# Waits by tile instead of by pool at the seams of a one-core adaLN block, forward and backward

## Chip, core and metric

The kernel runs on one core of one Trainium2 chip. A core has four compute engines that matter here (TensorE, called PE; VectorE, DVE; ScalarE, ACT; GpSimd, POOL), a fifth, SyncE (SP), that only issues transfers, and 16 DMA engines that move data between HBM and the on-chip SBUF. Matmuls write to PSUM, which has eight banks of 2 KB for each of the 128 partitions. The metric is the device time of one execution in microseconds (us), as the median of several runs.

## The reference

One transformer block whose two branches are modulated by a condition vector c, and its gradients. In bf16, with S = 2048 tokens, D = 512, 32 heads of 16, F = 1792:

```python
def forward(x, wqkv, wo, w1, b1, w2, b2, c, w_mod):
    sa, ca, ga, sb, cb, gb = split(silu(c) @ w_mod, 6)     # six rows of 512
    h = layernorm(x) * (1 + ca) + sa
    x = x + ga * attention(h, wqkv, wo)                    # softmax(q k^T / 4) v, 32 heads, no mask
    h = layernorm(x) * (1 + cb) + sb
    x = x + gb * (relu(h @ w1 + b1) ** 2 @ w2 + b2)
    return x

out, vjp = jax.vjp(forward, ...)
return out, *vjp(grad_out)       # out and the nine gradients
```

## The kernel before, in words

The work runs in five stages, one after the other, on tokens in four chunks of 512.

*Prep* (function `prep`, PSUM pool `psP`): loads, layer norm of x, the modulation rows `modbc`, and the projections of the first heads' q, k and v, with `pk`, `pm` and others as PSUM tiles and `vP` as an evicted piece of v that goes into `vaug` (v with a column of ones).

*Attention forward* (the loop over `u` in `range(NF + 2)`, PSUM pools `psS`, `psO` and `psM`): 512 units, each of one query chunk, one group of four heads and one tile of 128 keys. PE makes scores of four heads in two pairs of banks (`psST`), ACT takes their exponential (`ET`), and two units later PE multiplies with `vaug` into `oacc`. Into these units everything else of the first three chunks is woven: projection, both halves of the MLP, their gradients, weight gradients. A dictionary `plan` holds for each unit the functions to be called in it; `at(u, f, ...)` writes an entry, and `later(k, f, ...)` puts a transfer off by k steps. All products of this kind share one PSUM bank: `mm()` takes the only tile `pm` of `psM`. `last_ds(fc)` is one of them: in units 119 to 132 it makes fourteen products of `gfT` with `w2T`, each evicted by DVE into `ds`. `racc` holds five rows, of which rows 0 and 1 get the reciprocals of rows 1 and 4 of `modbc`; SP stores them to `rows_st` in HBM. `chunk_loads` and `ffinish` end a chunk: sums `r_inv` over heads, a scaling of `O_un` into `O_c`, and transposes of `O_c` (`ptC`).

*Last chunk* (`last_chunk`, PSUM pool `psM2`): MLP forward and backward of the fourth query chunk. Weight gradients are made as chains of products into one of three banks `pc`, added to a part that was stored before and written out; the last of these chains leaves `dwlast`. `dltT` is the transposed row sum of dO times O of this chunk; `store_grad` stores it to `d_st`.

*Attention backward* (SBUF pools `phIt`, `phIe`, `phIw`, `phIs1`, `phIg`, `qz1pool`; PSUM pools `psId`, `psIx`): 8 groups of four heads by 64 units of 512 keys and 128 queries. For each unit PE makes scores again, one head at a time, into three banks (`psS_A`, `psS_B`, `psS_C`), ACT takes `E_u` from them, PE makes dP into `psD_u`, DVE multiplies the two into `dS_u`, and PE sums dv and dk in `accVK` and, by way of transposes `dsT`, dq in `dqacc`. Where PE would wait, a product named `idle` is put in, whose result isn't used.

*Last stage* (`phJlow`, `phJbig`, `phJw`, `psJt`, `psJd`, `psJw`): gradient of the first layer norm's output, of wqkv, and of the modulation.

The order of instructions on every engine is written out by hand in all these stages (`tc.manual_schedule`), with SP's and POOL's in the last one in part left to the framework. What the framework puts in everywhere are the waits between engines.

Memory is taken in pools, which are opened and closed like brackets. A pool that is opened after another was closed may get the same bytes. The framework then lets the new user wait for the old ones. By default it does so by pool: a pool that lands on bytes of closed pools waits, at the first use of any of its tiles, for all users of those pools.

Of the kernel before, what the change touches and what calls it, by code (L numbers as in the profile page):

```python
# [34 lines left out]
def kernel(  # L35
# [18 lines left out]
    DVE = nc.vector  # L54
# [17 lines left out]
    modbc = persist.tile([P, 6, D], BF, name="modbc")  # L72
# [9 lines left out]
    rows_st = dram.tile([8, D], F32, name="rows_st")  # L82
# [57 lines left out]
        for to, fro in row_loads(*args):  # L140
            SP.dma_start(out=to, in_=fro)

    vaugpool = tc.alloc_tile_pool(name="vaugp", bufs=1, side="right")
    vaug = vaugpool.tile([P, TT, H + 1, DH + 1], BF, name="vaug")
    kts = [vaugpool.tile([P, n], BF, name=f"kt_sb{i}") for i in range(2)]
    qts = [vaugpool.tile([P, 512], BF, name=f"qt_sb{i}") for i in range(2)]

    with ExitStack() as ph:
        wk = ph.enter_context(tc.tile_pool(name="phC", bufs=2))
        ffw = ph.enter_context(tc.tile_pool(name="ffw", bufs=1))  # L150
        cb = ph.enter_context(tc.tile_pool(name="phMc", bufs=1))
        att = ExitStack()
        ework = att.enter_context(tc.tile_pool(name="phCe", bufs=4))
# [116 lines left out]
        def next_chain():  # L270
            dwq.pop(0)[2]()
# [490 lines left out]
        psp = {}  # L762
# [411 lines left out]

        fqueue = list(range(QC - 1))
        with ExitStack() as ph2:
            psp["p"] = ph2.enter_context(tc.tile_pool(name="psP", bufs=1, space=bass.MemoryType.PSUM))
            with tc.manual_schedule(engines={PE.engine, ACT.engine, DVE.engine, SP.engine, POOL.engine}):
                prep()
        plan_tasks()  # L1180
        stages = [*range(4, 14), *range(4), 30, 31, *range(14, 25)]
        with ExitStack() as ph2:
            pools["s"] = ph2.enter_context(tc.tile_pool(name="psS", bufs=3, space=bass.MemoryType.PSUM))
            pools["o"] = ph2.enter_context(tc.tile_pool(name="psO", bufs=1, space=bass.MemoryType.PSUM))
            pools["mm"] = ph2.enter_context(tc.tile_pool(name="psM", bufs=1, space=bass.MemoryType.PSUM))
            with tc.manual_schedule(engines={PE.engine, ACT.engine, DVE.engine, SP.engine, POOL.engine}):
                fh[0, 0] = (qts[0], kts[0])
                for u in range(NF + 2):
                    unit[0] = u
                    run_due()  # L1190
                    if u < NF:
                        if funits[u][2] == 4 and u + TT < NF:
                            fload(*funits[u + TT][0:2])
                        fscore(u)
                    if 2 <= u:
                        fpv(u - 2)
                    if u % 4 == 2 and u // 4 < len(stages):
                        later_stage(stages[u // 4])
                    if u % 4 == 0 and 18 <= u // 4 < 32:
                        turn_weights(u // 4 - 18)  # L1200
                    count, begun_group = products[0], open_group[0]
                    for f, args in plan.pop(u, ()):
                        f(*args)
                    if u < NF - 4:
                        step(u)
                    elif dwq and u >= NF - 2:
                        next_chain()
                    if products[0] == count and not (begun_group or open_group[0]):
                        steady(u - 2)
                    if u >= NF - 7 and "L" in loads and "O" not in loads["L"]:  # L1210
                        early_finish()
                    if u == NF:
                        tiny = wk.tile([P, 1], F32, name="tiny", tag="tiny", bufs=1)
                        ACT.activation(tiny[:], onesf[:, 0:1], AF.Sqrt)
                    if not dense and fqueue and fdone and u - 2 >= fdone[0][0]:
                        fqueue.pop(0)
                        qc, rr, ou = fdone.pop(0)[1:]
                        ffinish(qc, rr, ou, chunk_loads(qc))
                while dense:
                    unit[0] += 1  # L1220
                    run_due()
                    step(unit[0])

        strm, hsets = [], []

        def head_set(i):
            strm.append(tc.alloc_tile_pool(name=f"phIs{i}", bufs=1, side="right"))
# [298 lines left out]
        keep = {}  # L1526
        final[0] = True
        with ExitStack() as ph2:
            pools["mm"] = ph2.enter_context(tc.tile_pool(name="psM2", bufs=4, space=bass.MemoryType.PSUM))
            with tc.manual_schedule(engines={PE.engine, ACT.engine, DVE.engine, SP.engine, POOL.engine}):  # L1530
                pools["rs"] = pools["mm"].tile([P, 512], F32, name="rsums", tag="rs", bufs=1)
                DVE.memset(pools["rs"][:], 0.0)
# [10 lines left out]
                for i in range(4):  # L1543
                    fetch_part(i)
                att.close()
                qzpool = tc.alloc_tile_pool(name="qzpool", bufs=1, side="right")
                qz = [qzpool.tile([P, TT, 4, 32], BF, name="qz0")]
                kpool = tc.alloc_tile_pool(name="kpool", bufs=1, side="right")
                dpool = tc.alloc_tile_pool(name="dpool", bufs=1, side="right")
                dwr = tc.alloc_tile_pool(name="dwr", bufs=1, side="right")  # L1550
# [17 lines left out]
        dwr.release()  # L1568

    KS_tok, dOs_tok = keep["KS"], keep["dOs"]  # L1570
    qz1pool = tc.alloc_tile_pool(name="qz1pool", bufs=1, side="right")
    qz.append(qz1pool.tile([P, TT, 4, 32], BF, name="qz1"))
    head_set(1)

    stg = tc.alloc_tile_pool(name="phIg", bufs=2, side="right")
    xs = {}

    def load_grads(key, i, tile_ap):
# [1 line left out]
        SP.dma_start(out=tile_ap, in_=(dQc if key == "dq" else dVKtP)[i])  # L1580

    with ExitStack() as ph:
        tpool = ph.enter_context(tc.tile_pool(name="phIt", bufs=3))
        ework = ph.enter_context(tc.tile_pool(name="phIe", bufs=4))
        wk = ph.enter_context(tc.tile_pool(name="phIw", bufs=2))
        psd = ph.enter_context(tc.tile_pool(name="psId", bufs=2, space=bass.MemoryType.PSUM))
        psx = ph.enter_context(tc.tile_pool(name="psIx", bufs=1, space=bass.MemoryType.PSUM))
# [15 lines left out]
        def at(j, f, *args):  # L1603
            todo.setdefault(j, []).append((f, args))
# [173 lines left out]
        with tc.manual_schedule(engines={PE.engine, ACT.engine, DVE.engine, SP.engine, POOL.engine}):  # L1778
# [49 lines left out]
        dq_last = hst[HG - 1]["dq"]  # L1828

    with ExitStack() as ph:  # L1830
        low = ph.enter_context(tc.tile_pool(name="phJlow", bufs=1))
        big = ph.enter_context(tc.tile_pool(name="phJbig", bufs=1))
        wk = ph.enter_context(tc.tile_pool(name="phJw", bufs=2))
        pst = ph.enter_context(tc.tile_pool(name="psJt", bufs=2, space=bass.MemoryType.PSUM))
        psd = ph.enter_context(tc.tile_pool(name="psJd", bufs=2, space=bass.MemoryType.PSUM))
        psw = ph.enter_context(tc.tile_pool(name="psJw", bufs=3, space=bass.MemoryType.PSUM))
# [168 lines left out]
        with tc.manual_schedule(engines={PE.engine, ACT.engine, DVE.engine}):  # L2005
            for i in range(2):
                rsums.append(pst.tile([P, D], F32, name="rsumJ", tag="ptq"))
            for t in range(TT):
# [4 lines left out]
                if t in (3, 5, 7, 9):  # L2013
                    i = 4 + (t - 3) // 2
# [92 lines left out]
```

## Time and profile before

| | before |
|---|---|
| median of 3 runs | 2475.41 us |
| these runs | 2471.93 to 2484.3 us |
| profiled execution, its own time | 2480.28 us |
| its span in the trace | 2478.5 us |
| mean granted TensorE clock | 0.984 |
| busy: PE, ACT | 2310.0 us, 2300.5 us |
| busy: DVE, POOL | 1845.9 us, 490.5 us |

The profile is one execution, recorded by the hardware; all its times count from the start of the span. A timeline row gives the start of an instruction (or of a run of alike ones, with xcount), its duration, engine and line, what it writes and reads, and in brackets the idle time of its engine just before it and what ended that idle time. A windows row gives, for a stretch of the span, the busy time of each engine in it, the clock that TensorE was granted (1.00 is full speed), the mean busy share of the 16 DMA engines and the rate of transfer. The page's list of chain shares follows the work that ended last backwards and says which engine held it.

### The profile page before, as it was taken

To read this page: it belongs to the slowest core of one execution; us is meant where nothing else is said; L and a number is where in the kernel's file an instruction comes from. 1 tells how busy PE (TensorE), PEld (TensorE's weight loads), DVE (VectorE), ACT (ScalarE), POOL (GpSimd) and SP (SyncE) were. 2 spreads that over 40 slices of the span, in tenths; PEclk is the share of its full clock that TensorE was granted. 3 is DMA by queue.
4 is the path that set the end of the run, shared out by engine and by line. 5 is a ranking of instruction groups with operands and counts; after the bars stand their busy time and mean duration, and the time that the engine had idled before them with its cause. 6 is when DMAs were issued, how large, how long until landed. Compare 5 with 4: busy or idle time off the path is not lost.

```text
span 2478.5 us, 49843 instructions
## 1 busy us (share of the span) xinstructions
PE 2310.0 (93%) x18908; PEld 778.3 (31%) x18994; DVE 1845.9 (74%) x2393; ACT 2300.5 (93%) x3559; POOL 490.5 (20%) x661
## 2 busy tenths in 40 slices
PE   8899899988998998889999999999999999999999
PEld 3232233323322332432233223333233332222344
DVE  6555453455445554668999999999999999999986
ACT  7999999999998999629999999999999999999964
POOL 2211222432544353201110101101011010110100
PEclk9999999999998999999999999999999999999999
DMA  4478554267647774989999999999999999999995
GB/s 148 129 170 193 175 142 101 84 173 133 91 93 155 149 138 99 233 236 175 195 196 202 209 192 206 205 211 203 201 202 206 208 203 200 204 191 221 200 260 181
DMA packets 1192304, 440.58 MB, mean 178 GB/s; under 512 B 1068284, under 2 KB 1161914, under 8 KB 1191551
## 3 DMA queue, kind: packets, MB, share of 16 engines
q1 hardware_dynamic: 1155214, 392.23, 80.6%
q0 software_dynamic: 19872, 27.09, 6.9%
q10 hardware_dynamic: 16976, 18.07, 3.1%
q8 instruction: 149, 2.44, 0.4%
q14 instruction: 93, 0.75, 0.1%
HBM read 98.83 MB, written 72.63 MB: 69 GB/s over the span
## 4 chain that ended last, share of the span: by engine, by line
ACT 41%; PE 37%; DVE 8%; issue 8%; DMA 4%; ACTq 1%; SPq 0%; POOL 0%; DVEq 0%; another core or an unknown queue 0%; POOLq 0%
ACT E_u L1634 25%; ACT ET L580 13%; PE dqacc L1736 4%; PE psST L578 3%; PE psS_A L1628 3%; PE accVK L1709 2%; ACT dsT L1821 2%; PE pm L234 2%; PE psS_B L1628 2%; PE oacc L594 2%; PE psS_C L1628 2%; PE pdh L1929 2%; PE pm L502 2%; PE pm L412 2%; PE accVK L1718 2%
## 5 line engine op out<-in xcount | busy, mean ns | idle before, releaser
L1650 DVE TENSOR_TENSOR dS_u<-psD_u,E_u 128x1024 bf16<-128x1024 f32 x1024 | 1185.6, 1218 | 76.6 <-PE psD_u L1648 25.3
L580 ACT ACTIVATE ET<-psST 128x1024 bf16<-128x1024 f32 x1024 | 941.9, 1232 | 17.5 <-PE psST L578 17.1
L1634 ACT ACTIVATE E_u<-psS_A 128x512 bf16<-128x512 f32 x768 | 507.5, 661 | 13.1 <-DMA d_st<-dltT 10.2
L1634 ACT ACTIVATE E_u<-psS_B 128x512 bf16<-128x512 f32 x768 | 501.0, 652 | 8.6 <-issue 2.4
L1648 PE MATMUL psD_u<-iv,ido 32*128 32x512 bf16 x2048 | 409.7, 388 | 0.1
L578 PE MATMUL psST<-qt_sb,kt_sb 32*128 32x512 bf16 x2048 | 314.0, 385 | 42.3 <-ACT ET L580 36.1
L1634 ACT ACTIVATE E_u<-psS_C 128x512 bf16<-128x512 f32 x512 | 332.9, 650 | 2.5 <-PE psS_C L1628 1.0
L1628 PE MATMUL psS_A<-ik,iq 32*128 32x512 bf16 x768 | 294.0, 383 | 16.5 <-ACT E_u L1634 5.8
L1628 PE MATMUL psS_B<-ik,iq 32*128 32x512 bf16 x768 | 295.4, 385 | 10.4 <-ACT E_u L1634 3.1
L1757 POOL TENSOR_TENSOR dQacc<-dQacc,dqtmp 128x512 f32<-128x512 f32 x64 | 81.2, 1269 | 849.7 <-ACT dqtmp L1752 849.7
L1628 PEld LDWEIGHTS <-iq 32*128 32x128 bf16 x2048 | 130.2, 91 | 314.0 <-issue 298.2
L1709 PE MATMUL accVK<-dS_u,qz 128*32 128x512 bf16 x2048 | 213.3, 388 | 0.6 <-DVE dS_u L1650 0.3
L594 PE MATMUL oacc<-ET,vaug 128*32 128x512 bf16 x2048 | 206.9, 394 | 3.9 <-DVE ostage L598 3.9
L1718 PE MATMUL accVK<-E_u,dOs_tok 128*16 128x512 bf16 x2048 | 204.0, 387 | 0.0
L1628 PE MATMUL psS_C<-ik,iq 32*128 32x512 bf16 x512 | 193.9, 379 | 4.4
L578 PEld LDWEIGHTS <-kt_sb 32*128 32x128 bf16 x2048 | 85.3, 91 | 321.0 <-issue 299.3
L1736 PE MATMUL dqacc<-dsT,KS_tok 128*32 128x512 bf16 x2048 | 146.1, 383 | 13.4 <-ACT E_u L1634 0.4
L252 DVE COPY part<-pm 128x512 f32<-128x512 f32 (+2 forms) x106 | 65.2, 615 | 121.2 <-PE pm L234 110.8
L1821 ACT ACTIVATE dsT<-ptT 128x1024 bf16<-128x1024 bf16 x126 | 142.3, 1130 | 8.8 <-PE ptT L1682 8.1
L1648 PEld LDWEIGHTS <-ido 32*128 32x128 bf16 x2048 | 104.8, 91 | 106.4 <-issue 100.7
L1709 PEld LDWEIGHTS <-qz 128*32 128x32 bf16 x2048 | 58.4, 94 | 178.3 <-issue 163.2
L1757 POOL TENSOR_TENSOR dQst<-dQacc,dqtmp 128x512 bf16<-128x512 f32 x31 | 39.4, 1270 | 266.5 <-ACT dqtmp L1752 256.3
(421 smaller groups left out, 2672.2 us busy)
## 6 DMA issues: line engine op xcount, KB each, us to landing
p_st<-part POOLq DMA_DIRECT2D x36, 256.0 KB, 4.6
kt_sb<-qkT_st POOLq DMA_DIRECT2D x124, 64.0 KB, 3.2
wA<-in_B_w_dram SPq DMA_DIRECT2D x28, 256.0 KB
wB<-w1T_st SPq DMA_DIRECT2D x21, 256.0 KB
wA<-w2T_st SPq DMA_DIRECT2D x21, 256.0 KB
wB<-in_B_w_dram SPq DMA_DIRECT2D x21, 256.0 KB
p_st<-part POOLq DMA_DIRECT2D x28, 192.0 KB, 4.9
p_st<-part SPq DMA_DIRECT2D x18, 256.0 KB
```

Source lines behind the costliest of these rows:

```text
L578: PE.matmul(ps[:, hi, :], kt_sb[r:r + 32, kt * P:(kt + 1) * P], qt_sb[r:r + 32, :], start=True, stop=True, tile_position=(r, 0))
L580: ACT.activation(ET[:, 2 * pair:2 * pair + 2, :], ps[:], AF.Exp, scale=SCALE)
L594: PE.matmul(oacc[32 * hq:32 * hq + 32, :], lhsT, ET[:, hq, :], start=(kt == 0), stop=(kt == TT - 1), tile_position=(0, 32 * hq), skip_grou ...
L1628: PE.matmul(psS[:], st["q"][r:r + 32, qt * P:(qt + 1) * P], st["k"][r:r + 32, kc * 512:kc * 512 + 512], start=True, stop=True, tile_positi ...
L1634: ACT.activation(bst[u][0][:, hq, :], sst.pop((u, hq))[:], AF.Exp, scale=SCALE)
L1648: PE.matmul(psD[:, hi, :], st["do"][r:r + 32, qt * P:(qt + 1) * P], st["v"][r:r + 32, kc * 512:kc * 512 + 512], start=True, stop=True, til ...
L1650: DVE.tensor_tensor(dS_u[:, 2 * pair:2 * pair + 2, :], psD[:], E_u[:, 2 * pair:2 * pair + 2, :], ALU.mult)
L1709: PE.matmul(cur["vk"][32 * hq:32 * hq + 32, :], hst[hg]["qz"][:, qt, hq, :], bst[u][1][:, hq, :], start=(qt == 0), stop=False, tile_positi ...
L1718: PE.matmul(acc[32 * hq:32 * hq + DH, :], dOs_tok[:, qt, (hg * 4 + hq) * DH:(hg * 4 + hq + 1) * DH], E_u[:, hq, :], start=False, stop=(qt ...
L1736: PE.matmul(acc[32 * hq:32 * hq + 32, :], KS_tok[:, kc * 4 + kt, h * DH:h * DH + 32], tT[:, :, hq * 4 + kt, :], start=(kt == 0), stop=(kt ...
L1757: POOL.tensor_tensor(dst2, dst, tmp[:], ALU.add)
L1821: ACT.activation(dst, pt[:], AF.Identity)
```

## The change

Two edits. The first gives every pool but the two permanent ones (`persist`, and `dram` in HBM) the argument `reuse_waits="tile"`. With it, a tile waits only for the users of those earlier tiles that lay on its own bytes (in PSUM: in its own bank), and not for all users of the closed pools. It is in 28 places; three of them:

```diff
-    vaugpool = tc.alloc_tile_pool(name="vaugp", bufs=1, side="right")
+    vaugpool = tc.alloc_tile_pool(name="vaugp", bufs=1, reuse_waits="tile", side="right")
...
-            pools["s"] = ph2.enter_context(tc.tile_pool(name="psS", bufs=3, space=bass.MemoryType.PSUM))
+            pools["s"] = ph2.enter_context(tc.tile_pool(name="psS", bufs=3, reuse_waits="tile", space=bass.MemoryType.PSUM))
...
-        ework = ph.enter_context(tc.tile_pool(name="phIe", bufs=4))
+        ework = ph.enter_context(tc.tile_pool(name="phIe", bufs=4, reuse_waits="tile"))
```

The pools are those named above, and `phC`, `ffw`, `phMc` and `phCe` (forward), `qzpool`, `kpool`, `dpool` and `dwr` (last chunk).

The second edit moves the two one-row reciprocals from units 130 and 132 to 134 and 136, and the store of their rows from unit 134 to 138:

```diff
             for r, j in enumerate((1, 4)):
-                at(130 + 2 * r, DVE.reciprocal, racc[0:1, r, :], modbc[0:1, j, :])
-            at(134, sp, rows_st[6:8, :].unsqueeze(0), racc[0:1, 0:2, :])
+                at(134 + 2 * r, DVE.reciprocal, racc[0:1, r, :], modbc[0:1, j, :])
+            at(138, sp, rows_st[6:8, :].unsqueeze(0), racc[0:1, 0:2, :])
```

The order of all other instructions on all engines is the same in the text of the kernel.

More of the change, by code (lines that the diff above doesn't have):

```diff
@@ L1176 @@
         with ExitStack() as ph2:
-            psp["p"] = ph2.enter_context(tc.tile_pool(name="psP", bufs=1, space=bass.MemoryType.PSUM))
+            psp["p"] = ph2.enter_context(tc.tile_pool(name="psP", bufs=1, reuse_waits="tile", space=bass.MemoryType.PSUM))
             with tc.manual_schedule(engines={PE.engine, ACT.engine, DVE.engine, SP.engine, POOL.engine}):
@@ L1182 @@
         with ExitStack() as ph2:
-            pools["s"] = ph2.enter_context(tc.tile_pool(name="psS", bufs=3, space=bass.MemoryType.PSUM))
-            pools["o"] = ph2.enter_context(tc.tile_pool(name="psO", bufs=1, space=bass.MemoryType.PSUM))
-            pools["mm"] = ph2.enter_context(tc.tile_pool(name="psM", bufs=1, space=bass.MemoryType.PSUM))
+            pools["s"] = ph2.enter_context(tc.tile_pool(name="psS", bufs=3, reuse_waits="tile", space=bass.MemoryType.PSUM))
+            pools["o"] = ph2.enter_context(tc.tile_pool(name="psO", bufs=1, reuse_waits="tile", space=bass.MemoryType.PSUM))
+            pools["mm"] = ph2.enter_context(tc.tile_pool(name="psM", bufs=1, reuse_waits="tile", space=bass.MemoryType.PSUM))
             with tc.manual_schedule(engines={PE.engine, ACT.engine, DVE.engine, SP.engine, POOL.engine}):
@@ L1226, in head_set @@
         def head_set(i):
-            strm.append(tc.alloc_tile_pool(name=f"phIs{i}", bufs=1, side="right"))
+            strm.append(tc.alloc_tile_pool(name=f"phIs{i}", bufs=1, reuse_waits="tile", side="right"))
             hs = {key: strm[i].tile([P, n], BF, name=f"i{key}{i}") for key in ("k", "v", "q", "do")}
@@ L1528 @@
         with ExitStack() as ph2:
-            pools["mm"] = ph2.enter_context(tc.tile_pool(name="psM2", bufs=4, space=bass.MemoryType.PSUM))
+            pools["mm"] = ph2.enter_context(tc.tile_pool(name="psM2", bufs=4, reuse_waits="tile", space=bass.MemoryType.PSUM))
             with tc.manual_schedule(engines={PE.engine, ACT.engine, DVE.engine, SP.engine, POOL.engine}):
@@ L1570 @@
     KS_tok, dOs_tok = keep["KS"], keep["dOs"]
-    qz1pool = tc.alloc_tile_pool(name="qz1pool", bufs=1, side="right")
+    qz1pool = tc.alloc_tile_pool(name="qz1pool", bufs=1, reuse_waits="tile", side="right")
     qz.append(qz1pool.tile([P, TT, 4, 32], BF, name="qz1"))
     head_set(1)
-    stg = tc.alloc_tile_pool(name="phIg", bufs=2, side="right")
+    stg = tc.alloc_tile_pool(name="phIg", bufs=2, reuse_waits="tile", side="right")
     xs = {}
@@ L1830 @@
     with ExitStack() as ph:
[L1831 to L1836, printed above, removed]
+        low = ph.enter_context(tc.tile_pool(name="phJlow", bufs=1, reuse_waits="tile"))
+        big = ph.enter_context(tc.tile_pool(name="phJbig", bufs=1, reuse_waits="tile"))
+        wk = ph.enter_context(tc.tile_pool(name="phJw", bufs=2, reuse_waits="tile"))
+        pst = ph.enter_context(tc.tile_pool(name="psJt", bufs=2, reuse_waits="tile", space=bass.MemoryType.PSUM))
+        psd = ph.enter_context(tc.tile_pool(name="psJd", bufs=2, reuse_waits="tile", space=bass.MemoryType.PSUM))
+        psw = ph.enter_context(tc.tile_pool(name="psJw", bufs=3, reuse_waits="tile", space=bass.MemoryType.PSUM))
         entry = tc.manual_schedule(engines={PE.engine, ACT.engine, DVE.engine, SP.engine})
```

24 lines of the change are left out of this document (12 added, 12 removed).

## The prediction

> **What bounds the kernel now.** I read the page first, then one table of windows, cut where the stages change hands, because the change acts only there.
>
> ```profile
> span 2478.5 us, 49843 instructions
> ...
> PE 2310.0 (93%) x18908; PEld 778.3 (31%) x18994; DVE 1845.9 (74%) x2393; ACT 2300.5 (93%) x3559; POOL 490.5 (20%) x661
> ...
> ACT 41%; PE 37%; DVE 8%; issue 8%; DMA 4%; ACTq 1%; SPq 0%; POOL 0%; DVEq 0%; another core or an unknown queue 0%; POOLq 0%
> ```
>
> PE and ACT are each busy 93% of the span, and the chain that ended last goes through them for 78%. The table of windows by stage (length, busy time of each engine, granted clock, DMA share, GB/s) shows where the other 7% lie:
>
> ```profile
> core 0: us, PE busy (x) PEld busy (x) DVE busy (x) ACT busy (x) POOL busy (x), PEclk, DMA share, GB/s
> 0.00:41.20 41.20, 30.74 (x190) 15.12 (x193) 26.82 (x79) 27.55 (x44) 13.70 (x38) 0.96 0.47 155
> 41.20:999.00 957.80, 868.40 (x6031) 287.49 (x6098) 485.24 (x954) 943.19 (x1026) 315.15 (x491) 0.99 0.61 135
> 999.00:1109.40 110.40, 97.51 (x572) 46.57 (x580) 76.98 (x180) 48.50 (x91) 13.10 (x26) 1.00 0.91 244
> 1109.40:1113.90 4.50, 0.00 (x0) 0.00 (x0) 0.00 (x0) 0.00 (x0) 0.00 (x0) 0.58 0.79 264
> 1113.90:2371.00 1257.10, 1210.92 (x11503) 377.86 (x11503) 1185.88 (x1025) 1227.58 (x2333) 147.31 (x106) 0.98 1.17 202
> 2371.00:2478.50 107.50, 102.38 (x619) 51.29 (x625) 70.95 (x157) 53.66 (x67) 1.27 (x1) 1.00 0.75 220
> ```
>
> The attention forward (41 to 999 us) is bound by ACT (943 of 958), the attention backward (1114 to 2371) by ACT, PE and DVE together (98, 96, 94%), the last stage by PE. Between last chunk and backward lie 4.50 us in which no engine does anything: that is the waiting for closed pools in its pure form. The change can give no more than the waits at the four borders (about 41, 1000, 1109 and 2371 us) plus what the reciprocals hold up.
>
> **The change part by part.** With waits by pool, the first tile of a pool that lies on released bytes waits for the last user of every pool there; with waits by tile, only for users of tiles on its own bytes (in PSUM, its own bank). These are a part of the old waits, and every engine's order stays as it was, so no wait is added; what can cost time is only what an earlier start collides with, or the clock.
>
> *Prep to forward, 41 us.* The timeline of PE and DVE:
>
> ```profile
> 41.23 0.30 DVE L834 COPY vaug<-vP 128x512 bf16<-128x512 bf16 x1
> 41.25 0.39 PE L578 MATMUL psST<-qt_sb,kt_sb 32*128 32x512 bf16 x4 [1.77 <-DVE vP L833]
> ...
> 42.66 0.69 DVE L833 CAST vP<-pm 128x512 bf16<-128x512 f32 x1 [1.12 <-PE pm L828]
> ...
> 43.40 1.02 PE L828 MATMUL pm<-wqkv_nat,h1T 128*128 128x512 bf16 x4 [0.20 <-DVE vP L833]
> ```
>
> The first scores wait 1.77 us for an eviction of the prep pool that isn't in their banks. That wait goes. What is late next: PE's product after it has to be evicted by DVE, which is occupied until 41.23 + 0.30 = 41.53; the eviction that began at 42.66 can begin there, 1.1 earlier, and the next product (43.40) follows it. I take **1.1**; bounds 0 (if ACT has enough of a backlog from other causes) and 1.77.
>
> *The reciprocals.* Two one-row reciprocals of 3.33 us each stand on DVE before and between the last evictions of the ds products:
>
> ```profile
> 281.82 3.33 DVE L1203 RECIPROCAL racc<-modbc 1x512 f32<-1x512 bf16 x1
> ...
> 285.08 0.62 DVE L1129 CAST ds<-pm 128x512 bf16<-128x512 f32 x1
> 285.75 1.02 PE L1127 MATMUL pm<-gfT,w2T 128*128 128x512 bf16 x4 [2.01 <-DVE ds L1129]
> 286.81 0.69 DVE L1129 CAST ds<-pm 128x512 bf16<-128x512 f32 x1 [1.11 <-PE pm L1127]
> 287.19 25.77 ACT L580 ACTIVATE ET<-psST 128x1024 bf16<-128x1024 f32 x28 [1.48 <-PE psST L578]
> 287.42 3.33 DVE L1203 RECIPROCAL racc<-modbc 1x512 f32<-1x512 bf16 x1
> ...
> 292.66 6.22 SPq L179 DMA_DIRECT2D wA<-in_B_w_dram  x6
> 293.48 0.96 DVE L677 RECIPROCAL r_inv<-pm 128x128 f32<-128x128 f32 x1 [2.73 <-PE psST L578]
> 294.47 4.42 DVE L621 TENSOR_TENSOR O_c<-O_un,r_inv 128x512 bf16<-128x512 bf16 x4
> ...
> 299.92 0.62 PE L350 MATMUL ptC<-identb,O_c 128*128 128x128 bf16 x8
> ```
>
> The first holds the eviction of product 12 until 285.08; there is one pm bank, so the next product waits 2.01, the scores behind it come late, and ACT, the bound here, stands 1.48. Moved behind product 13, they hold no eviction of a product. The gain is ACT's 1.48: **1.5** (0 to 2.0). What they can now hold up: the last ds eviction would end about 2 us sooner, an estimate of 285.5 from 286.81 + 0.69 less 2.01; the two then end at 285.5 + 6.66 = 292.2, and r_inv, with PE 1.5 to 2 earlier, is wanted at 291.5 to 292. At most 0.7 late, and the transposes of O_c come only at 299.92, 1.0 us after DVE's scaling has ended (294.47 + 4.42 = 298.89), which covers it; if that cover were gone, PE would stand 0.7. On SP, the row store moves behind the loads of g_c, wo_nat and x_c, which no longer wait for the second reciprocal; the store itself then waits until 292.2, and the next load behind it (wA) left at 292.66, so nothing there is later. POOL, which takes g_c, can only gain.
>
> *Forward to last chunk, 1000 us.*
>
> ```profile
> 999.98 0.81 PE L659 MATMUL pm<-wo_nat,OT 128*128 128x512 bf16 x2 [0.65 <-DVE part L252]
> 1000.17 0.48 DVE L1532 MEMSET rsums<- 128x512 f32 x1 [0.25 <-DVE part L252]
> ```
>
> PE waits 0.65 for an eviction out of another bank; DVE does that eviction and the memset anyway. I take **0.4** (0 to 0.65).
>
> *Last chunk to backward, 1109 us.*
>
> ```profile
> 1108.65 0.37 PE L1628 MATMUL psS_A<-ik,iq 32*128 32x512 bf16 x1 [0.95 <-DVE dwlast L238]
> ...
> 1108.98 0.39 PE L1797 MATMUL idle<-identb,ones_bf 128*128 128x512 bf16 x1
> ...
> 1111.85 1.72 SPq L179 DMA_DIRECT2D d_st<-dltT  x4
> ...
> 1113.92 0.60 ACT L1634 ACTIVATE E_u<-psS_A 128x512 bf16<-128x512 f32 x1 [10.22 <-DMA d_st<-dltT]
> ...
> 1114.57 0.58 PE L1628 MATMUL psS_A<-ik,iq 32*128 32x512 bf16 x1 [5.20 <-ACT E_u L1634]
> ```
>
> The first exponential waits until the store out of dltT has landed. By the tiles' sizes in the order of allocation the first E_u lies on the tail of dwbuf and on woT, the first dS_u on rT and sT, and dltT below both, so by tile it needn't wait for that store. psS_A lies in the bank of the last pc chain: its 0.95 for dwlast stays, and the score is there at 1108.65 + 0.37 = 1109.02. ACT starts 1113.92 − 1109.02 = **4.9** earlier; PE's 5.20 go with it. dltT's store then runs beside the first units.
>
> The second half of this border is the clock. Windows of all engines around it, and far behind it one more fall:
>
> ```profile
> 1110.10:1113.50 3.40, 0.00 (x0) 0.00 (x0) 0.00 (x0) 0.00 (x0) 0.00 (x0) 0.50 0.81 262
> 1113.50:1127.10 13.60, 12.18 (x61) 2.25 (x60) 8.93 (x8) 9.33 (x18) 8.80 (x5) 0.50 0.49 113
> ...
> 1195.40:1205.60 10.20, 10.20 (x66) 2.94 (x66) 6.56 (x7) 7.86 (x14) 0.00 (x0) 0.50 0.88 165
> ```
>
> and windows of the dS_u product on DVE alone, the pace of the backward (length, busy, clock, DMA share, GB/s):
>
> ```profile
> 1115.30:1137.90 22.60, 17.90 (x15) 0.74 0.73 145
> 1137.90:1195.40 57.50, 55.14 (x48) 1.00 1.16 197
> 1195.40:1217.50 22.10, 17.87 (x17) 0.77 1.00 186
> 1217.50:2370.60 1153.10, 1094.63 (x947) 0.99 1.18 203
> ```
>
> The granted clock is 0.50 from 1110.1 to 1127.1. In the first 22.60 us DVE is idle 4.70; at the normal pace (1 − 1094.63/1153.10 = 5.07%) it would be 1.15. The slow clock and the first filling cost 3.55; I count **3.3** as the clock's. With the gap closed, PE goes on from its last idle-filling product (to 1108.98 + 0.39 = 1109.37) to the second psS_A when the first exponential of 0.60 has ended, at 1109.62, so the clock should stay. Bounds: 0, if the clock falls all the same (it fell 0.7 us behind the last matmul), and 3.55.
>
> [...]
>
> *Backward to last stage, 2371 us.* The queue's own waits, and a window:
>
> ```profile
> SPq L1847 <- PE accVK L1718: 5.3, 1, 5.3
> 2375.50:2389.00 13.50, 13.45 (x169) 9.63 (x163) 8.10 (x16) 8.26 (x10) 1.27 (x1) 1.00 0.90 292
> ```
>
> SP's load of wT stands 5.3 us for the last E_u product, but PE is busy 13.45 of the 13.50 us after it with transposes and the last dq sums: that work hides the load. wT_all also lies on the dS_u buffers used last, so most of the wait stays. **0**; bound 0 to the 0.05 that PE is idle there. Were the cover gone, it would be 5.3.
>
> Sum: 1.1 + 1.5 + 0.4 + 4.9 + 3.3 = **11.2 us**. The profiled execution took 2480.28 (span 2478.5 and 1.8 around it), 4.87 over the median of the runs, 2475.41; none of the terms scales with that difference, so 2475.41 − 11.2 = **2464.2**.
>
> **The rivals.**
>
> *The clock falls at 1110 all the same.* For it: it fell 0.7 us after the last matmul, and at 1195.4 with PE busy 10.20 of 10.20, so idleness isn't its only cause. Against: from 1137.90 to 1195.40, without a pause, it was 1.00. Gain 11.2 − 3.3 = 7.9: 2467.5.
>
> *The fall at 1195 goes as well.* If that one is an after-effect of the cold start, it vanishes with it. Its price: 22.10 − 17.87 = 4.23 idle against 5.07% of 22.10 = 1.12, so 3.1. Gain 14.3: 2461.1. Against: 68 us lie between them.
>
> *The option does nothing,* because the allocator can't follow the users of these tiles one by one and keeps the pool's waits. Only the reciprocals are left: 2475.41 − 1.5 = 2473.9. Against: each border's waiting names one single instruction, so users are followed.
>
> *Slower: falls of the clock like that of 1195 become frequent.* The backward then runs on other phases of whatever grants the clock, and without a pause that stands between dense stretches. Each fall costs 3.1; three (9.3) still leave a gain, four (12.4) outweigh 11.2 and give 2476.6, eight give 2489. For it: such a fall came with PE wholly busy. Against: the clock is 0.99 over the 1153 us after it.
>
> **How the numbers follow.** The forecast has 0.44, the clock falling anyway 0.25, the second fall gone too 0.17, the option without effect 0.08, more falls 0.06. I take 0.5% (12.4 us: below 2463.0, above 2487.8) as about what a measurement of this kernel can tell from no change; the runs shown spread over 12.4 us (2471.93 to 2484.3), so a median of such runs can stand some 4 us off its case. Faster by over 0.5%: three quarters of the 0.17, some four tenths of the 0.44, a little of the 0.25: 0.33. Slower by over 0.5% needs eight falls: 0.03. The rest is 0.64. The range goes from 14.3 and upper bounds of the small terms (1.77 + 2.0 + 0.65 instead of 3.0, so 1.4 more), with the 4 us of scatter, 2456, up to the option without effect, 2474; outside lie the more falls and half of the case at its upper edge.
>
> **What would show it.** Right: the first E_u at 1109 to 1110 less what was gained before, with no wait for d_st; PEclk 1.00 in the windows from 1110 to 1127; no window without any busy engine; DVE's evictions of products 12 and 13 without a reciprocal in front, and ACT's 1.48 gone near 287; the first scores at 39.5 instead of 41.25. Wrong: a clock of 0.50 in the start of the backward (then 7.9), the first E_u still waiting for a DMA (the address is not what I worked out: then 4.9 and 3.3 go), r_inv or the transposes of O_c waiting for a reciprocal, or a mean clock in the backward below 0.98.

## The result, and the profile after

| | before | after |
|---|---|---|
| median of 22 runs each | 2475.43 us | 2468.83 us |
| these runs | 2467.43 to 2487.63 us | 2460.11 to 2480.18 us |
| profiled execution, its own time | 2480.28 us | 2464.45 us |
| mean granted clock of it | 0.984 | 0.990 |

The ratio is 0.9972, with a 95% interval of 0.9958 to 0.9985: 6.9 us faster, between 3.7 and 10.4. The two profiled executions lie 15.8 us apart, over twice as much, so the first question is which part of that the change made. The page and the windows by stage of the changed kernel (same columns as before):

```profile
span 2462.6 us, 49825 instructions
...
PE 2300.2 (93%) x18908; PEld 777.6 (32%) x18994; DVE 1846.0 (75%) x2393; ACT 2298.3 (93%) x3559; POOL 488.9 (20%) x661
```
```profile
core 0: us, PE busy (x) PEld busy (x) DVE busy (x) ACT busy (x) POOL busy (x), PEclk, DMA share, GB/s
38.60:996.60 958.00, 867.92 (x6033) 287.40 (x6099) 487.56 (x958) 943.64 (x1027) 314.36 (x491) 0.99 0.60 135
996.60:1106.30 109.70, 96.83 (x571) 46.41 (x578) 77.09 (x179) 48.16 (x90) 13.19 (x27) 1.00 0.90 242
1106.30:2358.00 1251.70, 1204.33 (x11525) 378.69 (x11523) 1187.16 (x1027) 1227.16 (x2334) 146.90 (x106) 0.99 1.18 204
2358.00:2462.60 104.60, 100.57 (x596) 50.09 (x602) 69.19 (x154) 51.84 (x65) 1.28 (x1) 1.00 0.73 218
```

No stretch without any busy engine is left between last chunk and backward. Cut at the starts of single instructions that both kernels have, the 15.84 us come from these stages (each row is the time, in us, from the mark of the row above to its own):

| up to | before | after | difference |
|---|---|---|---|
| start, first exponential ET | 41.73 | 39.06 | −2.67 |
| last ET | 954.81 | 954.91 | +0.10 |
| eviction of rsums (L1521) | 110.69 | 110.64 | −0.05 |
| first exponential E_u | 6.69 | 1.74 | −4.95 |
| 31st product dS_u | 42.27 | 40.73 | −1.54 |
| last product dS_u | 1213.22 | 1206.56 | −6.66 |
| end | 109.08 | 109.01 | −0.07 |

The border at 1109 us, now at 1106, by the timeline:

```profile
1104.61 0.68 DVE L1521 COPY r_inv<-rsums 97x512 f32<-97x512 f32 x1
1105.21 0.68 DVE L238 TENSOR_TENSOR dwlast<-pc,part 128x512 bf16<-128x512 f32 x1
```
```profile
1105.94 0.37 PE L1628 MATMUL psS_A<-ik,iq 32*128 32x512 bf16 x1 [0.86 <-DVE dwlast L238]
...
1107.00 0.37 PE L1628 MATMUL psS_A<-ik,iq 32*128 32x512 bf16 x1 [0.34 <-ACT E_u L1634]
```
```profile
1106.35 0.60 ACT L1634 ACTIVATE E_u<-psS_A 128x512 bf16<-128x512 f32 x1 [4.88 <-DMA dOT<-dOs_c]
```
```profile
1109.83 1.73 SPq L179 DMA_DIRECT2D d_st<-dltT  x4
```

The first E_u starts 0.04 us behind the end of its score (1105.94 + 0.37); the transfer that the row names landed in the same instant (in e8, where the score is earlier, E_u is too). The store of dltT is issued 3.5 us after that start, so nothing waits for it any more. What is left is the wait for dwlast in the score's own bank. Windows of all engines behind it show the clock:

```profile
1106.30:1110.90 4.60, 3.46 (x22) 0.95 (x19) 2.36 (x2) 4.09 (x8) 4.60 (x3) 1.00 0.96 319
1110.90:1117.70 6.80, 6.66 (x41) 1.25 (x35) 5.84 (x5) 4.46 (x9) 3.95 (x3) 0.50 0.57 146
```

The clock falls in the first units all the same (a fall is a stretch with a granted clock of 0.50), for 6.8 us instead of 17.0. At the first border and at the reciprocals (timelines of PE, DVE and ACT):

```profile
39.53 0.39 PE L578 MATMUL psST<-qt_sb,kt_sb 32*128 32x512 bf16 x2 [0.51 <-DVE vP L833]
...
41.67 1.02 PE L828 MATMUL pm<-wqkv_nat,h1T 128*128 128x512 bf16 x4 [0.46 <-DVE vP L833]
```
```profile
283.66 0.69 DVE L1129 CAST ds<-pm 128x512 bf16<-128x512 f32 x1 [1.11 <-PE pm L1127]
284.27 6.54 DVE L1203 RECIPROCAL racc<-modbc 1x512 f32<-1x512 bf16 x2
290.74 0.95 DVE L677 RECIPROCAL r_inv<-pm 128x128 f32<-128x128 f32 x1
```
```profile
269.56 40.66 ACT L580 ACTIVATE ET<-psST 128x1024 bf16<-128x1024 f32 x44
```

Instead of 1.77 the scores wait 0.51, for the eviction of vP, which the profile names as what released them; and ACT's run of 44 exponentials has no gap where 1.48 stood.

### The profile page after: what moved, and what is told of

The parts are those of the page before. It is cut to its first block, busy times and chain, and to the rows that moved or that the text cites. A ratio compares the mean times of both kernels' runs of the same rounds, so it can differ in the third digit from the quotient of the medians.

```text
span 2462.6 us, 49825 instructions
## 1 busy us (share of the span) xinstructions
PE 2300.2 (93%) x18908; PEld 777.6 (32%) x18994; DVE 1846.0 (75%) x2393; ACT 2298.3 (93%) x3559; POOL 488.9 (20%) x661
## 4 chain that ended last, share of the span: by engine, by line
ACT 41%; PE 36%; DVE 8%; issue 8%; DMA 4%; ACTq 1%; POOL 0%; DVEq 0%; SPq 0%; another core or an unknown queue 0%; POOLq 0%
ACT E_u L1634 25%; ACT ET L580 13%; PE dqacc L1736 5%; PE psST L578 3%; PE psS_A L1628 3%; PE accVK L1709 2%; PE pm L234 2%; ACT dsT L1821 2%; PE psS_B L1628 2%; PE oacc L594 2%; PE psS_C L1628 2%; DMA dsT<-dS_u 2%; PE pdh L1929 2%; PE pm L502 2%; PE pm L412 2%
```

## The experiments

Each kernel is compared with the kernel before, in runs on the same chip. In the traces I read the same marks as in the table above.

**e1: the reciprocals alone**

```diff
-                at(130 + 2 * r, DVE.reciprocal, ...)      # waits by pool everywhere, as before
+                at(134 + 2 * r, DVE.reciprocal, ...)
```

> Waits by pool everywhere; only the two reciprocals and their store are moved. Theory (the gain is a sum of fixed waits at the borders, on top of which falls of the clock scatter): ACT's 1.48 us near 287 us goes, the lead over the kernel before steps by about 1.5 there and nowhere else; the first E_u still waits about 10 us; the time is 1.5 us less than before, within the scatter. Rival (what counts is how many falls of the clock an execution happens to get, and any small shift of time changes that): the step at 287 is the same, but the backward is as much changed as in the full change.

Measured: 2475.73 us, ratio 0.9997 (0.9984 to 1.0010). Timelines of ACT near the reciprocals, and at the border:

```profile
275.40 30.82 ACT L580 ACTIVATE ET<-psST 128x1024 bf16<-128x1024 f32 x33
...
1111.75 0.60 ACT L1634 ACTIVATE E_u<-psS_A 128x512 bf16<-128x512 f32 x1 [10.71 <-DMA d_st<-dltT]
```

ACT's gap is gone, and the lead over the kernel before, read at the same ET, steps there from −0.3 to 1.6, by 2.0 where the theory has 1.5 (in the changed kernel from 1.2 to 2.9, by 1.7). The time shows nothing of it; an interval from −4.0 to +2.5 us can neither exclude nor confirm it.

**e2: the tile waits alone**

```diff
+                at(130 + 2 * r, DVE.reciprocal, ...)      # waits by tile everywhere, as in the changed kernel
-                at(134 + 2 * r, DVE.reciprocal, ...)
```

> Waits by tile everywhere, reciprocals where they were. Theory: leads as in the full change, about 2.3 us at 41 us and 5.0 at 1109 with some 1.6 of the clock's behind it, but no step at 287: 1.5 less gain than the full change, 5 to 7 us in the median. Rival (the reciprocals had to be moved because the tile waits make them late): the full 6.9 or more is lost.

Measured: 2466.34 us, ratio 0.9971 (0.9953 to 0.9988), so 7.2 us. ACT's gap is back (2.47 instead of 1.48; the clock is at 0.50 just there and DVE waits 1.61 instead of 1.11 for the product before it, which may make it longer), and the border at 1109 is as in the changed kernel:

```profile
287.44 18.45 ACT L580 ACTIVATE ET<-psST 128x1024 bf16<-128x1024 f32 x20 [2.47 <-PE psST L578]
```

The tile waits don't need the moved reciprocals: the rival falls. The whole gain is there without them.

**e3: tile waits behind the last chunk only**

```diff
-    qz1pool = tc.alloc_tile_pool(name="qz1pool", bufs=1, side="right")
+    qz1pool = tc.alloc_tile_pool(name="qz1pool", bufs=1, reuse_waits="tile", side="right")
...                                                     # and every pool opened after it; all before it by pool
```

> Waits by tile only for the pools opened after the last chunk. Theory: no lead until 1109, then 5.0 us at the first E_u and 1 to 2 more of the clock in the first 23 us of the backward: about 6 us in all. The granted clock is 0.50 for about 7 us behind the start instead of 17. Rival (the clock falls for as long as before): 5.0 alone.

Measured: 2467.99 us, ratio 0.9973 (0.9958 to 0.9989), 6.7 us.

```profile
1109.93 0.60 ACT L1634 ACTIVATE E_u<-psS_A 128x512 bf16<-128x512 f32 x1 [6.71 <-PE psS_C L1628]
```

From the eviction of rsums to the first E_u it takes 1.74 us, as in the full change; the clock falls at 1112.9 for 10.2 us, and the 31st product comes after 41.86 us against 42.27. This one border carries what can be measured.

**e4: tile waits up to the last chunk only**

```diff
-            pools["s"] = ph2.enter_context(tc.tile_pool(name="psS", bufs=3, space=bass.MemoryType.PSUM))
+            pools["s"] = ph2.enter_context(tc.tile_pool(name="psS", bufs=3, reuse_waits="tile", space=bass.MemoryType.PSUM))
...                                                     # and every pool opened up to dwr; reciprocals as before
```

> Waits by tile only for the pools opened up to the last chunk, reciprocals not moved. Theory: a lead of 2.3 us at 41 us, of which falls of the clock in the forward leave 1 to 2.3, up to 0.6 more at 1000 us, and nothing at 1109, where the first E_u waits about 10 us for the store out of dltT as before: 1 to 3 us in all. Rival (the tile waits of the last chunk's own pools also bring dltT's store forward): the wait at 1109 shrinks too.

Measured: 2477.81 us, ratio 1.0005 (0.9992 to 1.0018).

```profile
1110.60 0.60 ACT L1634 ACTIVATE E_u<-psS_A 128x512 bf16<-128x512 f32 x1 [11.59 <-DMA d_st<-dltT]
```

The border at 1109 is untouched (7.67 from the eviction of rsums). In the trace the lead at the ETs is 0.6 behind the first border and stays between 0.1 and 0.7 up to 770 us. It is 1.6 at the last ET, but it gets there at about 780 us, behind a fall that lasts 3.4 us instead of 6.8, and at about 850, where no border lies. The time shows no gain; the interval reaches from 2.0 faster to 4.5 slower.

**e5: PE kept working through the old wait**

```diff
                     if c == "s" and b < NU // 4:
+                        if b == 0 and i == 3:
+                            for _ in range(22):
+                                PE.matmul(idle[:], ...)       # in the kernel before
```

> The kernel before (waits by pool), with 22 products named idle put on PE in front of the fourth score, so that PE works through the wait for the store out of dltT. ACT's wait of about 10 us stays as it is. Theory of the prediction (the clock falls because PE pauses, and 3.3 us of the border are the clock's): the clock stays at 1.00 past 1110, the 30 products of dS_u after the first E_u come 1.5 to 3.3 us sooner than before (42.3 us there). Rival (the fall isn't PE's pause but the thin work of the first units, which it has in the changed kernel too): PE's clock falls about 7 us later than before, at the first units, and stays low for 7 to 10 us; the gain is 0 to 1.5. In neither case is the whole gain of the change reached.

Measured: 2475.74 us, ratio 0.9987 (0.9970 to 1.0003). Timeline of PE and windows of all engines:

```profile
1107.22 4.91 PE L1792 MATMUL idle<-identb,ones_bf 128*128 128x512 bf16 x22
```
```profile
1108.80:1117.60 8.80, 6.39 (x32) 2.20 (x32) 2.36 (x2) 4.05 (x8) 4.46 (x3) 1.00 0.60 199
1117.60:1124.40 6.80, 6.49 (x41) 1.23 (x35) 5.84 (x5) 4.50 (x9) 4.33 (x3) 0.50 0.49 92
```

With PE busy up to 1112.1 the fall comes 7.5 us later than before, at 1117.6, and the way from the first E_u to the 31st product takes 40.97 instead of 42.27: 1.3 less. That is the rival's case. The fall doesn't need the long pause, of which 1.6 us are left here (1112.1 to 1113.7); it comes in the first units.

**e6: denser first units**

```diff
-                        if b < 2 and i % 2 == 1:
-                            if nq > 0:
-                                keep_warm()
-                            elif nq < 0:
-                                PE.matmul(idle[:], ...)
+                        if b < 2 and i % 2 == 1 and nq > 0:
+                            keep_warm()
+                        elif b == 0 and nq < 0:
+                            for _ in range(2):
+                                PE.matmul(idle[:], ...)       # in the changed kernel
```

> The changed kernel with two products named idle at each exponential of the first ten instead of one at every second (15 more). Rival of e5 (thin work of the first units drops the clock): with the denser work there is no fall near 1111, and the first 30 products after the first E_u take about 39.5 us instead of 40.7: 1.2 less. Theory of the prediction (a pause of PE drops it, and the changed kernel has no pause left): the fall that it still has at 1110.9 has another cause, it comes all the same, and the added products cost up to 3 us.

Measured: 2469.01 us, ratio 0.9966 (0.9952 to 0.9980).

```profile
1107.30:1110.90 3.60, 3.60 (x21) 1.02 (x18) 1.23 (x1) 2.66 (x5) 3.60 (x3) 1.00 0.77 267
1110.90:1117.70 6.80, 6.36 (x47) 1.71 (x47) 5.66 (x5) 5.21 (x10) 4.08 (x3) 1.00 0.55 179
```

No fall: ahead of 1110.9 PE is busy 3.60 of 3.60 us here, against 3.46 of 4.60 in the changed kernel, so thin work of PE in the first units is its cause. (e12 has the same added products and no fall at the start either; the twelve other traces all have one.) But 40.38 us to the 31st product is only 0.35 less than in the changed kernel, where 1.2 were expected: either the added products cost part of what the clock gives, or there was less to give. The start is never faster than this in any trace, 1.9 below the 42.27 before. How much of the 3.55 us lost there before was the clock's can be estimated from the eight traces without products added behind the first E_u and with the old order: their starts take 40.7 to 42.3 us and grow with the time at half clock, 6.8 to 17.1 us, and a straight line through them has 40.2 at no fall. That gives some 2 us for the clock, an estimate; the rest would be the filling of the pipeline.

**e7: a step of the dq sums moved into the thin stretch**

The reason for it is the falls in the backward. These are windows of the dS_u product on DVE (length, busy and count, clock), cut at the beginnings of the falls, in the kernel before and in e1:

```profile
1277.40:1413.90 136.50, 129.56 (x113) 0.99 1.18 204
1413.90:1434.40 20.50, 18.46 (x17) 0.92 1.11 194
1434.40:1745.00 310.60, 296.27 (x257) 0.99 1.20 203
1745.00:2018.00 273.00, 259.23 (x225) 0.99 1.19 205
```
```profile
1485.60:1506.10 20.50, 18.53 (x17) 0.92 1.20 190
1506.10:1584.60 78.50, 74.13 (x65) 0.98 1.16 203
1584.60:1721.10 136.50, 129.52 (x113) 0.99 1.19 205
```

The counts, less the one cut in two at an edge, are 112, 16, 256, 224 and 16, 64, 112: all multiples of 16, which is a pair of blocks: these falls come at one point of the pair. In the nine profiles with the old order of the backward, 54 of the 60 falls there do. Two come one product earlier, behind the 63rd (the one at 1195 before, and one in e4), and four lie elsewhere, behind windows in which PE itself was busy only 33 to 67%. At the common point PE's busy share doesn't tell why; the windows of all engines before a fall and in it:

```profile
1270.60:1274.00 3.40, 3.33 (x40) 0.94 (x40) 3.40 (x4) 3.33 (x7) 1.17 (x1) 1.00 1.16 217
1274.00:1277.40 3.40, 3.28 (x29) 1.00 (x26) 3.23 (x4) 3.40 (x8) 0.10 (x1) 0.99 1.21 138
1277.40:1280.80 3.40, 3.40 (x22) 1.08 (x20) 2.79 (x3) 2.86 (x5) 0.00 (x0) 0.50 1.13 250
```

In the window before the fall PE is busy 3.28 of 3.40 us, but with 29 products instead of 40.

```diff
-            "e5 s6 q s7 D s8 e6 e7 d1 e8 s9 D d2 e9 q Q s10 "
-            "s11 e10 D q s12 e11 e12 s13 ... ").split(), "CBACBACBABABCABC"
+            "e5 s6 q s7 D s8 e6 e7 d1 e8 s9 D e9 q s10 "
+            "s11 e10 D d2 q s12 Q e11 e12 s13 ... ").split(), "CBACBACBABABACBC"
```

> The changed kernel with one step of the dq sums (8 products of 128 rows) moved one dS_u later in every second block of the backward, and the score banks relettered for it. In the six profiles so far almost all falls of the clock in the backward begin 3.4 us after the same point of a pair of blocks, where the work of PE is thinnest. Theory (falls come when the window in which the clock is judged happens to lie on that stretch; how many an execution gets is chance of phase, and makes the scatter): the falls at that point vanish, the scatter shrinks to a few us, and the median comes down by 4 to 8 us, unless the moved step costs PE waits of its own. Rival (falls have a cause outside the work of PE): as many falls as before, elsewhere; no gain.

Measured: 2579.72 us, ratio 1.0407 (1.0368 to 1.0447). PE's longest waits, and a window over the backward:

```profile
PE psS_C L1628 <- ACT E_u L1634: 26.5, 62, 0.4
PE psS_C L1628 <- ACT dqtmp L1752: 10.5, 47, 0.5
```
```profile
1149.50:2437.00 1287.50, 1209.08 (x10827) 362.21 (x10824) 1127.29 (x964) 1180.61 (x2197) 133.24 (x97) 0.92 1.07 186
```

A failure: scores in the relettered banks wait for ACT in nearly every pair of blocks (62 and 47 times in 64 pairs), and falls become many and long (0.92 over the backward). As two things were changed at once, it decides nothing on the falls' cause.

**e8: another bank for the first score**

```diff
+            psx.tile([P, 512], F32, name="first", tag="ps0")     # takes bank 4; accVK and idle get bank 5
             idle = psx.tile([P, 512], F32, name="idle", tag="accVK")
```

> The changed kernel with the bank of psS_A exchanged against that of accVK and idle, so that the first score doesn't lie in the bank of the last weight-gradient chain. Theory (what is late next at this border is that bank): psS_A's wait of 0.86 for dwlast goes, the first E_u starts 0.8 to 0.9 earlier, and no more, since the score's operands are there; 0.9 less in the trace, not to be seen in the time. Rival (another operand is late, such as the transfer that ends at the same instant): E_u starts where it did.

Measured: 2467.23 us, ratio 0.9959 (0.9943 to 0.9974).

```profile
1103.09 0.39 PE L1628 MATMUL psS_A<-ik,iq 32*128 32x512 bf16 x1
1104.02 0.38 PE L1798 MATMUL idle<-identb,ones_bf 128*128 128x512 bf16 x1 [0.54 <-DVE dwlast L238]
```

The score waits no longer, the idle product does. From the eviction of rsums (1102.69) to the first E_u (1103.51) it takes 0.8 us instead of 1.7: the theory's 0.9.

**e9, e10, e11: products added in the thin stretch**

```diff
-            "s11 e10 D q s12 e11 e12 s13 e13 D q s14 s15 e14 e15 D q "        # kernel of e8
+            "s11 e10 D q s12 e11 e12 s13 e13 D q s14 f s15 e14 e15 D q "      # e9: f is keep_warm()
+            "s11 e10 D q s12 e11 e12 s13 e13 D f q s14 f s15 e14 e15 D q "    # e11
...
-            "s5 s6 e5 f f t2 e6 s7 T2 e7 D s8 e8 D f f s9 e9 q q s10 "
+            "s5 s6 e5 f f t2 e6 s7 T2 e7 D s8 e8 D f s9 e9 q q s10 "          # e10, with e9's line
```

> The kernel of e8 with one more keep_warm product (128 rows, adds zero) in every second block of the backward, in the middle of the thin stretch: 64 products of 0.2 to 0.39 us. e7 didn't decide what makes the falls there, because the moved step made PE wait. Theory (the judged window is too thin there, by little): no falls that begin 3.4 us behind that point, the backward after its start takes 1200 us and some 0 to 13 for the added products, in every execution, so a smaller scatter. Rival (it isn't how much PE does there): falls as before, 3 to 10 of them, and 0 to 13 us more.

> As e9, but one of the four keep_warm products of the other block is taken out for it, so that PE's work is that of the kernel of e8. Theory: the falls at the old point vanish, nothing is added, about 1200 us for the backward after its start, 6 to 9 us less than the changed kernel in the median, unless the other block was kept up by just that product, and the falls come there instead. Rival: no difference to e8.

> As e9 with two products more instead of one. Theory: no falls at the old point, as e9, and twice its price for PE's time (0 to 26 us). If one product is too little to lift the stretch, this one shows it by fewer falls than e9. Rival: falls as before.

| | median, range | ratio | last 993 products of dS_u |
|---|---|---|---|
| e8 | 2467.23 (2460.85 to 2471.73) | 0.9959 (0.9943 to 0.9974) | 1205.0 us |
| e9 | 2462.22 (2459.38 to 2465.64) | 0.9943 (0.9925 to 0.9961) | 1206.4 us |
| e10 | 2462.67 (2459.02 to 2465.68) | 0.9946 (0.9928 to 0.9963) | 1206.7 us |
| e11 | 2469.07 (2467.22 to 2472.93) | 0.9974 (0.9959 to 0.9989) | 1213.5 us |

Windows of the dS_u product in e9, and in e11:

```profile
1147.80:2289.90 1142.10, 1089.49 (x942) 1.00 1.19 204
2289.90:2293.30 3.40, 1.30 (x2) 0.50 1.14 251
```
```profile
1143.00:2350.00 1207.00, 1146.28 (x988) 1.00 1.17 203
```

No fall is left at the old point. The one fall in e9 and the one in e10 begin elsewhere (PE had been busy 59% and 51% of the window before them), and in e11 there is none.

One trace without such falls could be luck, since the nine with the old order have 2 to 10 falls each. The traces tell more. All falls of a trace begin on a grid of 3.413 us (to 0.001 us), so the edges of the windows that brought no fall are known too. In the nine traces with the old order 230 edges lie behind the 16th product dS_u of a pair. All 54 that come 0.58 to 0.80 us after its start begin a fall, and none of the 176 others does. Only one edge in e9 falls into this stretch, and just at its border, so e9's trace alone shows nothing. e10 has five edges in it, e11 three, e12 (below) two, and none of these ten begins a fall. So the falls there do come from what PE does in that stretch; which property of its work counts, the number of products or another, stays open.

The runs agree. The mean granted clock is 0.990 to 0.994 in all 29 runs of e9 to e12, against 0.981 to 0.992 in the 22 of the changed kernel, and e9's and e10's runs (six each) lie within 7 us, where those 22 spread over 20. The price is the other half of the theory: e11's second product costs 7.1 us in the trace (0.11 each), and the fit below puts e9's first at some 5. Moving instead of adding shows no saving in e10 (6 above the fit), but e12, with e10's order, has 1203.3 us, only 2 above it: single traces don't settle this price.

**e12: e6, e8 and e10 together**

> The changed kernel with e6 (two idle products at each of the first ten exponentials), e8 (bank of psS_A) and e10 (one keep_warm product moved into the thin stretch) together. Theory: the three act in different places and add: E_u 0.9 us behind the eviction of rsums instead of 1.7, no fall of the clock near the start and 40.4 us instead of 41.7 to its 30th product, no falls at the thin stretch: 1.3 us less than e10, a median of about 2461, and as small a scatter as e9's and e10's. Rival (the start's clock isn't worth anything, as e6 against the changed kernel): as e10.

Measured: 2459.79 us (2458.18 to 2460.39), ratio 0.9924 (0.9910 to 0.9938).

```profile
1102.90:1113.10 10.20, 9.40 (x56) 2.50 (x55) 6.63 (x7) 7.67 (x14) 7.44 (x5) 1.00 0.75 233
1113.10:1123.10 10.00, 9.85 (x78) 2.73 (x77) 9.12 (x9) 8.64 (x17) 1.41 (x1) 1.00 1.14 184
```

It is 0.76% or some 19 us below the kernel before and clear of the changed kernel, whose interval begins at 0.9958. 1.0 us to the first E_u where 0.9 were expected, no fall at the start; but 41.4 to the 31st product, where 40.4 were expected, so the start's clock brought e12 little in its trace. Whether it is ahead of e10 is open, since their intervals overlap.

## Why the prediction was right

It gave 2464.2 and 2456 to 2474; 2468.83 lies inside, 4.6 above. The way and the main term were right, a second term was not, and the range held because the rival without that term was in it. In the traces the terms come to 0.95 + 1.7 + 0 + 4.95 + 1.5 = 9.1 instead of 11.2, of which the forward gives some back. Point by point, by its own steps:

- **The border at 1109: right.** 4.9 predicted, 4.95 measured between the same two instructions, and e3, e2 and the changed kernel all have 1.74 there. The addresses were read rightly (E_u doesn't lie on dltT), and so was what stays: the 0.95 for dwlast, now 0.86. e3 and e4 show that this border alone makes the measurable gain.
- **The clock of the start: the term that was mis-sized, 3.3 against 1.5.** The step that failed is "With the gap closed, PE goes on ... so the clock should stay", an estimate of mine from the pause of some 0.25 us that would be left there (1109.37 to 1109.62). The pause is 0.34 in the trace, and the clock fell at 1110.9 all the same, with PE busy 3.46 of 4.60 us and no pause of PE over 0.86 us between the last chunk and the fall. e5 and e6 show why: the first units are too thin in themselves (in e5 the clock falls at 1117.6 behind 6.39 busy of 8.80 us), and with them thickened the clock stays at 1.00 (e6, 3.60 of 3.60). And the 3.55 us of the first 22.60 had been put down to the clock nearly whole, though only some 2 were, by the estimate at e6. The rival "the clock falls at 1110 all the same" is what happened, and its 2467.5 is the nearest of all figures given.
- **The first border: right in size, 1.1 against about 0.95.** The second pm product starts at 41.67 instead of 43.40; 0.78 of that the profiled execution had in hand before the border, as its last pk product already ended that much earlier. That the scores would still wait 0.51 for vP wasn't foreseen.
- **The reciprocals: right in the trace (1.5 against 1.7, and 2.0 in e1), not visible in the time.** r_inv wasn't late: it follows the reciprocals at 290.74, and the transposes of O_c weren't held up.
- **The border at 1000 us: 0.4 against nothing.** PE's and DVE's short waits are gone, but PE's wait for O_c a few products later grows from 0.31 to 0.98 and takes them up: the stage takes 110.64 instead of 110.69. In the other traces it takes 108.0 to 112.2, so a single pair of traces couldn't show 0.4 either way.
- **The border at 2371: right in its worth, wrong in the wait.** That most of SP's 5.3 us would stay didn't come: the load of wT now waits 0.5, and it is the next load in the queue (qz) that waits 4.3 for the same product. The last stage takes 109.01 instead of 109.08, so the earlier load was worth nothing, as said.
- **What the forward gives back.** From the first ET to the last the changed kernel takes 0.10 more, although 1.7 of the reciprocals' are in it. 0.37 are lost at the third exponential, and its clock falls at 80.0, where the kernel before had no fall. Of the ten traces with tile waits there seven have a fall at 80 to 83 us, of the four with pool waits one (e3): whether the change brings it stays open.

The rest of the 15.8 us is chance. In the backward after its start the two profiled executions differ by 6.66 us; the clock stood at 0.50 for 37.5 us of it before and 17.1 after. Over the nine profiles with the old orders (e7 and e9 to e12 left out) the length follows this time:

| | half clock, us | last 993 products, us |
|---|---|---|
| e2 | 6.8 | 1201.0 |
| e8 | 13.7 | 1205.0 |
| after | 17.1 | 1206.6 |
| e4 | 23.9 | 1211.4 |
| e5, e1 | 30.7, 30.7 | 1211.8, 1213.5 |
| e3, e6 | 34.1, 34.1 | 1212.1, 1211.6 |
| before | 37.5 | 1213.2 |

A straight line through them has 1199.8 us at no fall and 0.39 us per us, 1.3 for each fall of 3.4 us, and no point is over 2.4 off it. These nine executions have from 2 to 10 falls, by where the windows of the clock lie against the blocks, and by the line that alone spreads the stage by 12 us. The runs without a profile agree: over the 22 of the changed kernel, time and mean granted clock go together (correlation −0.89).

Whether the fall at 1195 of the kernel before, for which a rival asked 3.1, was an after-effect of the cold start stays open. e1 has the cold start (13.7 us) and no such fall. But the two traces whose cold start lasts 17.1 us, before and e4, both have one, 85.3 us behind its beginning. There the windows lie alike against the work, and the fall comes close to the usual point of a pair, so the position may be all there is to it.

The rival "slower", more falls in the backward, didn't come, though its mechanism is real: e7 shows falls making a kernel 4% slower (mean clock 0.92 over the backward), together with the waits of PE there. The prediction missed that such falls were there already: behind the one at 1195 the kernel before has eight more of 3.4 us, which a mean clock of 0.99 over 1153 us hides.

## What to carry to other kernels

Where a stage change leaves all engines idle, look at what the first instruction behind it waits for and whether it lies on the same bytes: a pool's wait can hang on a store that has nothing to do with the new tile, and here only that one border of four was worth something that the runs can show. Where a wait is taken away, look for the next one that takes it up: at 1000 us PE's 0.65 went, its wait for O_c a few products later grew from 0.31 to 0.98, and the stage stayed at 110.64 against 110.69. If one execution's profile shows far more than the runs do, compare the same stage in several profiles before explaining it.

## What the runs showed of the hardware

- The clock falls not only in pauses. It fell with PE recorded as busy 3.28 of 3.40 us (before, at 1277.4), in 54 of 60 cases at the same point of the kernel's cycle, and with one 128-row product more in that stretch per 19.5 us (e10, e12) or two (e11) it did so at none of ten edges. The recorded busy time alone is no measure of what keeps the clock up: in the same trace a window with 3.20 busy of 3.40 us, from 1280.8 on, brought no fall.
- Falls last 3.4 us or multiples of it (3.413, 6.827, 10.240 and 17.067 us before), and from fall to fall lie whole numbers of windows of 3.413 us. The windows lie differently against the work from trace to trace: with the same order in the backward, the falls at the common point come behind the 16th product dS_u of pairs 8, 15, 16, 32, 46, 53, 54 and 58 before, and of pairs 32, 39, 40 and 42 in the changed kernel. As time and granted clock go together in the runs (−0.89 over the 22 of the changed kernel), the falls are likely most of their scatter.
- A fall of 3.4 us cost 1.3 us here by the line above. Half of 3.4 us, 1.7, is an estimate of what a clock of 0.50 takes from PE alone; the stage lost less, in a stretch that PE, ACT and DVE bound together (96, 98 and 95% busy in the changed kernel).
